# Partial sums of a chunked matmul: two of four groups start on empty PSUM banks and are added in DRAM

## The chip, the cores and the metric

One Trainium2 chip, one of its cores. A time is device microseconds of one execution of the whole program; the time of a kernel is the median over its runs. One execution was also profiled, and all rows below come from that one.

## The reference, cut to what matters

Sigmoid attention (4 batches, 12 heads, 448 tokens, head size 64) gives 1792 tokens of 768. Two feed-forward blocks follow, all in float32:

```python
rms = np.sqrt(np.mean(x * x, axis=-1, keepdims=True) + 1e-06)
xn = x / rms * rms_g                                 # 1792 x 768
g, val = xn @ w_gate, xn @ w_val                     # 768 -> 1536
x = (g / (1 + np.exp(-g)) * val) @ w_out             # 1536 -> 768
h = x @ w_in2                                        # 768 -> 2048
out = (h - np.tanh(h)) @ w_out2                      # 2048 -> 768
```

The last product, with `w_out2`, is the one that the change touches.

## The kernel before

Activations lie transposed: a tile holds 128 features by the 448 tokens of one batch. Float32 values are split into a high and a low part, and a product of one 128x128 weight block with one tile is three matmuls of 448 columns (high x high, high x low, low x high). TensorE's order in the feed-forward part is fixed in the text: all its pieces are in one stream ("moe"). The phases are A (gate and value), B (`w_out`), C (`w_in2`) and D (`w_out2`). A and C take two batches at a time with a seven-product scheme (line 734); B and D use line 769. The batches go in two pairs, (0, 1) and then (2, 3).

Phase D has 16 key chunks (features of the 2048) and 6 output chunks `m`. Its keys are cut into four groups of four (`GR["D"]`), because the activations of a group are made by the C pieces just before it and their tiles are used up before the next. So D runs as group 0, two C pieces, group 1, two C pieces, group 2, one C piece, group 3. For one pair of batches each group makes 6 x 2 partial sums of 128x448. The order inside a group is chunk `m` after chunk `m`, both batches side by side, one PSUM bank each.

- `prologue` (line 639) begins a sum. In group 0 it takes an empty bank. In a later group it loads the sum so far from DRAM (line 644, a transfer that SyncE issues, `unit<-sumD`) and `seed` (line 647) copies it into the bank: the copy runs on ScalarE or VectorE under line 279, as all plain copies do, and is shown as `ps<-unit`.
- The first matmul of a group starts the bank anew only in group 0 (`k < GR[ph]`); in the others it adds to the seed.
- `epilogue` (line 650) copies the bank to a unit in SBUF (line 279, `unit<-ps`). After groups 0 to 2 SyncE stores that to DRAM (line 657, `sumD<-unit`); after group 3 it goes to the output (line 660).

So there are 3 x 12 x 2 = 72 loads, seeds and stores of this kind in D. Phase B has two groups and 24 of each.

Everything is recorded as a piece of work with the engines that may do it and a cost for each, and the class `Plan` then chooses the engine and the order of issue. It walks through a model of the five engines' clocks, takes among the pieces that can start soonest the oldest one, and looks at most 500 pieces ahead (`WINDOW`). Buffers are handed out in that modelled order too: 74 units of 128x448 in SBUF and 8 PSUM banks. Each engine then runs its list strictly in order on the chip, waiting on semaphores for what a piece reads. A transfer's cost in the model is the time that the issuing engine is taken, and `after` the time from there to its landing. `pool` and `dve` (lines 272 to 276) also mark operations that the model does not let VectorE and GpSimd do at the same time (the flag behind the cost).

Other work that shares the engines in phase D: weight blocks of `w_in2` and `w_out2` are loaded (line 329), unpacked (lines 279 and 339), summed (385), split in two (279 and 350) and, for the second pair of batches, stored and reloaded (370 and 419). The results of C pass through `tanh` (685), a subtraction (686) and a split (279 and 635). From the last C piece of the first pair on, the normalised input of the second pair is made (`spread_norm`, `x_units`: 572, 576, 580, 623, 595, 600).

Of the kernel before, what the change touches and what calls it, by code (L numbers as in the profile page):

```python
# [15 lines left out]
ALU = mybir.AluOpType  # L16
# [3 lines left out]
B, H, S, D = 4, 12, 448, 64  # L20
# [5 lines left out]
GR = {"B": 6, "D": 4}  # L26
# [34 lines left out]
class Plan:  # L61
# [11 lines left out]
    def add(self, engines, run, reads=(), writes=(), stream=None, after=0):  # L73

        n = len(self.work)
        self.work.append((engines, run, tuple(reads), tuple(writes), stream, after))
        self.rank.append(n + self.later)
        for s, _ in (*reads, *writes):
            if not s.uses or s.uses[-1] != n:
                s.uses.append(n)  # L80
# [134 lines left out]
def tile_sigmoid_attention_moe_moe(  # L215
# [14 lines left out]
    nc = tc.nc  # L230
# [20 lines left out]
    add = plan.add  # L251
# [4 lines left out]
    def bank(kind="mm"):  # L256
        return slot(kind, ps_p, [P, 512], F32, "ps")

    def unit(kind, dt=F32):
        return slot(kind, unit_p, [P, S], dt, "unit")  # L260
# [4 lines left out]
    def keys(c):  # L265
        return [c["h"]["t"], c["l"]["t"]]


    def act(n, psum=False, ptr=False):
        return {"ACT": ((155 if psum else 195) + n / 1.2, False)}  # L270

    def dve(n, two=True, psum=True, fast=False):
        return {"DVE": ((150 if psum or fast else 210) + n / 0.96 / (2 if fast else 1), fast or (two and not psum))}
# [4 lines left out]
    def copy(engines, to, of, reads, writes):  # L278
        add(engines, lambda e: (nc.scalar.copy if e == "ACT" else nc.vector.tensor_copy)(to(), of()), reads, writes)  # L279
# [323 lines left out]
    def right_units(ph, bs, i, x):  # L603

        f = {}
        split_of = lambda n: lambda: right_split(ph, bs, n, i, f[n])

        def of(e, names):
            f.update(zip(names, (x[b, 2 * i + e] for b in bs)))

        def total(n, a, b):
            f[n] = right_sum(f[a], f[b])

        return ([lambda: (of(0, ("B11", "B12")), split_of("B11")()), lambda: total("T1", "B12", "B11"), split_of("T1")],
                [lambda: (of(1, ("B21", "B22")), split_of("B21")()), lambda: total("T2", "B22", "T1"), split_of("T2"),
                 lambda: total("T3", "B22", "B12"), split_of("T3"), lambda: total("T4", "B21", "T2"), split_of("T4"), split_of("B22")])
# [11 lines left out]
    ps_t, gs_t, sums_t = {}, {}, {}  # L628
    last_group = lambda ph: {"B": KF1, "D": KF2}[ph] // GR[ph] - 1

    def parts(t):
# [4 lines left out]
            c["l"].tile, t.tile, c["h"].tile.bitcast(F32)), [t["t"], kh], [kl])  # L636
        return c

    def prologue(ph, bs, m, g):
        for b in bs:  # L640
            ps = ps_t[ph, b, m] = bank("m2")
            if g:
                d, a = sums_t.pop((ph, b, m)), unit("acc")
                add({"SP": (650, False)}, lambda e, a=a, d=d: nc.sync.dma_start(out=a.tile, in_=d.tile), [d["t"]], [a["t"]], after=2000)
                seed(ps, a, False)

    def seed(to, of, psum):
        copy({**act(S, psum=psum), **dve(S)}, lambda: to.tile[:, :S], lambda: of.tile[:, :S], [of["t"]], [to["t"]])

    def epilogue(ph, bs, b, m, g):  # L650
        ps = ps_t.pop((ph, b, m))
        last = g == last_group(ph)
        a = unit("sum" if last else "st")
        copy({**act(S, psum=True), **dve(S)}, lambda: a.tile, lambda: ps.tile[:, :S], [ps["t"]], [a["t"]])
        if not last:
            d = sums_t[ph, b, m] = Slot(None, lambda: dram_p.tile([P, S], F32, name=f"sum{ph}{b}_{m}_{g}"))
            add({"SP": (650, False)}, lambda e: nc.sync.dma_start(out=d.tile, in_=a.tile), [a["t"]], [d["t"]], after=2000)
            return
        if ph == "D":
            add({"SP": (650, False)}, lambda e: nc.sync.dma_start(out=out[b, m], in_=a.tile), [a["t"]], [], after=2000)  # L660
            return
        xg[b, m] = a
        if b == bs[-1]:
            if m % 2 == 0:
                halves["C", bs, m // 2] = right_units("C", bs, m // 2, xg)
            for u in halves["C", bs, m // 2][m % 2]:
                u()
# [82 lines left out]
    def job_units(j):  # L750

        ph, bs, _, blocks = jobs[j]
        if blocks is None:
            return seven_units(j)

        def one(n, k, m):
            w = whls[j]
            first, last = k % GR[ph] == 0, k % GR[ph] == GR[ph] - 1
            if first:
                prologue(ph, bs, m, k // GR[ph])  # L760
            pss = [ps_t[ph, b, m] for b in bs]
            acs = [acts[ph, b, k] for b in bs]
            part = lambda p: w.tile[:, "hl".index(p), n * P:(n + 1) * P]

            def block(e):
                hi, lo = part("h"), part("l")
                for i, (wt, p) in enumerate(((hi, "h"), (hi, "l"), (lo, "h"))):
                    for ps, a in zip(pss, acs):
                        nc.tensor.matmul(  # L769
                            ps.tile[:, :S], lhsT=wt, rhs=a[p].tile,  # L770
                            start=first and i == 0 and k < GR[ph], stop=last and i == 2, skip_group_check=True)

            add({"PE": (3 * len(bs) * MM, False)}, block,
                [w["h"], w["l"], *[k for a in acs for k in keys(a)]], [ps["t"] for ps in pss], stream="moe")
            if last:
                for b in bs:
                    epilogue(ph, bs, b, m, k // GR[ph])

        return [lambda n=n, k=k, m=m: one(n, k, m) for n, (k, m) in enumerate(blocks)]
# [170 lines left out]
```

## Time and profile before

| | |
|---|---|
| median of 3 runs | 1110.64 us (1110.25 to 1111.54) |
| the profiled execution | 1111.01 us |
| its span in the trace | 1109.2 us |

The span runs from the first to the last instruction of the program in the trace; 1.8 us of the profiled execution lie outside it. "Busy" is the union of an engine's instructions; register, wait and transfer-issuing instructions do not count as busy, except that what GpSimd issues stands under POOL. PE is TensorE, PEld its weight loads, DVE is VectorE, ACT is ScalarE, POOL is GpSimd, SP is SyncE, and a "q" behind an engine's name is its sequencer.

### The profile page before, as it was taken

Reading aid. Unit: us, or ns where it says so; the run is one execution under the profiler, and the core shown is the slowest. Engines: PE = TensorE matmul, PEld = TensorE weight load, DVE = VectorE, ACT = ScalarE, POOL = GpSimd, SP = SyncE. Lnnn points to the kernel's source line nnn. Section 1 sums busy time; section 2 is a strip of 40 time slices with the busy share of each in tenths; the row PEclk is TensorE's granted clock in tenths of the full one; section 3 lists DMA queues with packets and bytes.
Section 4 is the critical chain, followed back from the end, with each engine's and each line's share of the span. In section 5 each row is a group of like instructions: output and inputs, shape, how many; then the busy total and the mean of one; then the engine's idle time right before and its main releaser. Section 6 shows DMA issues by size and latency. Waiting matters only on the chain.

```text
span 1109.2 us, 14723 instructions
## 1 busy us (share of the span) xinstructions
PE 1092.8 (99%) x5364; PEld 914.3 (82%) x5364; DVE 701.0 (63%) x1075; ACT 503.2 (45%) x896; POOL 149.6 (13%) x108
## 2 busy tenths in 40 slices
PE   9999999999999998999999999999999999999998
PEld 3333338999999997999998888999899989999997
DVE  0353816877478789767698966633666686474651
ACT  5776864443255346355364533312344353243431
POOL 0000003300021000123132001200021021222100
PEclk9999999999999999999999999999999999999999
DMA  5774554469668546599899563334344135656432
GB/s 163 246 221 114 143 177 179 146 253 316 212 207 282 208 157 232 181 321 364 288 345 320 192 198 119 115 121 135 103 164 147 57 103 159 195 179 199 146 116 100
DMA packets 92456, 211.40 MB, mean 191 GB/s; under 512 B 25312, under 2 KB 58080, under 8 KB 92384
## 3 DMA queue, kind: packets, MB, share of 16 engines
q1 hardware_dynamic: 92080, 210.30, 56.3%
q8 instruction: 42, 0.69, 0.3%
q14 instruction: 30, 0.25, 0.1%
q10 hardware_dynamic: 304, 0.16, 0.1%
HBM read 137.68 MB, written 72.74 MB: 190 GB/s over the span
## 4 chain that ended last, share of the span: by engine, by line
PE 94%; DVE 4%; issue 1%; ACT 1%; DMA 0%; POOL 0%; DVEq 0%; ACTq 0%; POOLq 0%
PE ps L734 42%; PE ps L769 37%; PE ps L490 7%; PE ps L520 7%; DVE unit L279 1%; DVE wt L350 1%; DVE unit L635 1%; PE ps L286 1%; DVE unit L708 0%; ACT unit L279 0%; DVE unit L681 0%; PE ps L554 0%; DMA wC<-cv 0%; ACT wt L279 0%; DVE unit L600 0%
## 5 line engine op out<-in xcount | busy, mean ns | idle before, releaser
L734 PE MATMUL ps<-unit,wt 128*128 128x448 f32 x2520 | 521.5, 366 | 9.6 <-DVE unit L708 5.4
L734 PEld LDWEIGHTS ps<-unit,wt 128*128 128x128 f32 x2520 | 471.4, 188 | 55.7 <-DVE unit L708 6.9
L769 PE MATMUL ps<-unit,wt 128*128 128x448 f32 x2016 | 413.9, 365 | 1.1 <-ACT wt L279 1.1
L769 PEld LDWEIGHTS ps<-unit,wt 128*128 128x128 f32 x2016 | 378.1, 188 | 33.1 <-ACT wt L279 1.5
L279 ACT COPY unit<-ps 128x448 f32<-128x448 f32 x172 | 91.2, 534 | 329.0 <-PE ps L769 200.5
L279 DVE COPY unit<-ps 128x448 f32<-128x448 f32 x80 | 49.9, 624 | 129.8 <-PE ps L769 124.0
L350 DVE TENSOR_TENSOR wt<-cv,wt 128x768 fp32r<-128x768 f32 (+1 forms) x111 | 101.7, 924 | 18.8 <-ACT wt L279 17.4
L279 ACT CAST wt<-cv 128x768 fp32r<-128x768 f32 (+1 forms) x97 | 75.1, 781 | 41.4 <-PE ps L734 16.3
L497 ACT ACTIVATE unit<-ps 128x448 f32<-128x448 f32 (+1 forms) x192 | 86.5, 547 | 5.9 <-PE ps L490 5.9
L635 DVE TENSOR_TENSOR unit<-unit 128x448 fp32r<-128x448 f32 x94 | 75.8, 807 | 7.4 <-ACT unit L279 4.7
L490 PE MATMUL ps<-wt 64*128 64x448 f32 (+1 forms) x384 | 78.9, 547 | 0.0
L520 PE MATMUL ps<-unit,vs 128*64 128x448 f32 (+1 forms) x384 | 77.7, 545 | 0.0
L350 POOL TENSOR_TENSOR wt<-cv,wt 128x768 fp32r<-128x768 f32 (+1 forms) x25 | 48.2, 1928 | 214.9 <-ACT wt L279 145.5
L708 DVE TENSOR_TENSOR unit<-ps,unit 128x448 f32<-128x448 f32 x84 | 51.9, 619 | 33.2 <-PE ps L734 23.7
L350 POOL TENSOR_TENSOR wt<-wt 128x768 fp32r<-128x768 f32 (+1 forms) x21 | 36.3, 1732 | 269.6 <-ACT wt L279 188.9
L279 ACT CAST wt<-wt 128x768 fp32r<-128x768 f32 (+1 forms) x60 | 44.8, 753 | 53.8 <-PE ps L734 38.0
L339 DVE SCALAR_TENSOR_TENSOR cv<-wt,zero 128x768 uint32<-128x768 uint32 x68 | 66.8, 982 | 2.5 <-ACT unit L535 0.7
L490 PEld LDWEIGHTS ps<-wt 64*128 64x128 f32 (+1 forms) x384 | 32.3, 173 | 43.3 <-issue 36.1
L520 PEld LDWEIGHTS ps<-unit,vs 128*64 128x64 f32 (+1 forms) x384 | 25.2, 136 | 49.1 <-issue 32.9
L279 ACT CAST zero<-wt 128x768 f16<-128x768 bf16 x49 | 53.1, 1083 | 26.6 <-DVE cv L339 19.8
L279 ACT CAST unit<-unit 128x448 fp32r<-128x448 f32 x91 | 51.3, 567 | 25.4 <-DVE unit L681 9.0
L350 DVE TENSOR_TENSOR wt<-wt 128x768 fp32r<-128x768 f32 (+1 forms) x59 | 51.4, 879 | 6.4 <-ACT wt L279 5.5
(49 smaller groups left out, 548.9 us busy)
## 6 DMA issues: line engine op xcount, KB each, us to landing
wt<-in_w_out SPq DMA_DIRECT2D x28, 768.0 KB, 5.9
sumD<-unit SPq DMA_DIRECT2D x72, 224.0 KB, 2.7
unit<-sumD SPq DMA_DIRECT2D x72, 224.0 KB, 4.7
wt<-in_w_in SPq DMA_DIRECT2D x16, 768.0 KB, 5.8
wC<-cv SPq DMA_DIRECT2D x32, 384.0 KB, 4.3
wt<-wC SPq DMA_DIRECT2D x16, 768.0 KB, 4.3
wt<-in_w_gate SPq DMA_DIRECT2D x12, 768.0 KB, 5.2
wt<-in_w_val SPq DMA_DIRECT2D x12, 768.0 KB, 5.4
```

What stands on the lines that cost most here:

```text
L279: add(engines, lambda e: (nc.scalar.copy if e == "ACT" else nc.vector.tensor_copy)(to(), of()), reads, writes)
L286: nc.tensor.matmul(ps[:, :S], lhsT=mark[:, :P], rhs=mark, start=True, stop=True)
L339: add(dve(NW, psum=False), lambda e: nc.vector.scalar_tensor_tensor(out=c.tile.bitcast(U32), in0=r.tile[:, :NW, 1], scalar=13, in1=z.tile, ...
L350: add({**dve(n, psum=False), **pool(n)}, lambda e: ENG[e].tensor_sub(lo(), of(), hi().bitcast(F32)), [*reads, *kh], [*kl])
L490: nc.tensor.matmul(ps[i, c].tile[:n, :S], lhsT=t.tile[rows, at:at + n], rhs=t.tile[rows, :S], start=True, stop=True)
L497: add(act(S, psum=True), lambda e: nc.scalar.activation(to.tile[at:at + n, :S], ps.tile[:n, :S], AF.Sigmoid, bias=-math.log(S), scale=1.0 ...
L520: nc.tensor.matmul(ps.tile[i * D:(i + 1) * D, :S], lhsT=v.tile[:n, c, i, :], rhs=a[c][i].tile[:n, :], start=(c == 0), stop=(c == 3))
L635: add({**pool(S), **dve(S, psum=False)}, lambda e: ENG[e].tensor_sub(c["l"].tile, t.tile, c["h"].tile.bitcast(F32)), [t["t"], kh], [kl])
L708: add(dve(S), lambda e: nc.vector.tensor_add(t.tile, ps.tile[:, :S], t.tile), [ps["t"], t["t"]], [t["t"]])
L734: nc.tensor.matmul(ps.tile[:, :S], lhsT=part(a), rhs=x[b].tile, start=n in ((1, 2, 5) if opening else (1, 5)) and i == 0 and q == 0, stop= ...
L769: nc.tensor.matmul(ps.tile[:, :S], lhsT=wt, rhs=a[p].tile, start=first and i == 0 and k < GR[ph], stop=last and i == 2, skip_group_check=True)
```

## The change

Groups 1 and 2 of phase D no longer load and seed the sum so far; their first matmul starts the bank anew, as in group 0. Their epilogue still copies the bank to a unit, and then GpSimd issues a transfer that adds the unit to the sum in DRAM (`accum_op=ALU.add`). Group 0's sum is stored as before, and group 3 loads the sum and seeds with it as before. In the model of `Plan` the adding transfer takes GpSimd for 1100 ns and lands 3000 ns later; a SyncE store takes 650 and 2000. Phase B, with two groups, is as it was, since its second group is its last.

```diff
+    def seeded(ph, g):
+        return g and (ph != "D" or g == last_group(ph))
+
     def prologue(ph, bs, m, g):
         for b in bs:
             ps = ps_t[ph, b, m] = bank("m2")
-            if g:
+            if seeded(ph, g):
                 d, a = sums_t.pop((ph, b, m)), unit("acc")
                 add({"SP": (650, False)}, lambda e, a=a, d=d: nc.sync.dma_start(out=a.tile, in_=d.tile), [d["t"]], [a["t"]], after=2000)
                 seed(ps, a, False)
@@ epilogue
         copy({**act(S, psum=True), **dve(S)}, lambda: a.tile, lambda: ps.tile[:, :S], [ps["t"]], [a["t"]])
+        if not last and g:
+            d = sums_t[ph, b, m]
+            add({"POOL": (1100, False)}, lambda e: nc.gpsimd.dma_start(
+                out=d.tile, in_=a.tile, accum_op=ALU.add), [a["t"], d["t"]], [d["t"]], after=3000)
+            return
         if not last:
@@ block, in one
-                            start=first and i == 0 and k < GR[ph], stop=last and i == 2, skip_group_check=True)
+                            start=first and i == 0 and not seeded(ph, k // GR[ph]), stop=last and i == 2, skip_group_check=True)
```

## Rows read from the trace of the kernel before

**Rows 1.** The page: busy time, share of the span and instructions by engine

```profile
PE 1092.8 (99%) x5364; PEld 914.3 (82%) x5364; DVE 701.0 (63%) x1075; ACT 503.2 (45%) x896; POOL 149.6 (13%) x108
```

**Rows 2.** Stretches of the span (us): busy and count by engine, clock, DMA share, GB/s

```profile
490.00:594.00 104.00, 104.00 (x513) 96.01 (x512) 80.47 (x122) 52.84 (x88) 28.03 (x16) 1.00 0.93 332
594.00:611.00 17.00, 15.48 (x74) 13.40 (x73) 16.57 (x25) 10.10 (x18) 6.32 (x4) 1.00 0.93 318
611.00:640.00 29.00, 27.85 (x137) 25.20 (x136) 27.34 (x48) 16.22 (x31) 0.00 (x0) 1.00 0.57 187
640.00:676.00 36.00, 34.60 (x169) 31.08 (x168) 25.31 (x37) 14.31 (x26) 3.68 (x2) 1.00 0.51 169
...
894.00:1067.00 173.00, 173.00 (x855) 160.03 (x854) 104.35 (x156) 62.84 (x110) 36.83 (x25) 1.00 0.52 169
```

**Rows 3.** Who TensorE waited for from 490 us on: total us, times, longest

```profile
PE ps L734 <- DVE unit L708: 1.5, 1, 1.5
PE ps L734 <- DVE unit L279: 1.4, 2, 0.7
PE ps L734 <- ACT unit L279: 1.2, 2, 0.6
PE ps L769 <- ACT wt L279: 1.1, 1, 1.1
```

**Rows 4.** Groups of instructions, 490 to 594 us: the seeds (count | busy, mean ns | idle before)

```profile
L279 ACT COPY ps<-unit 128x448 f32<-128x448 f32 x17 | 8.9, 534 | 3.4 <-DMA unit<-sumD 3.0 <-DVE unit L279 0.3
L279 DVE COPY ps<-unit 128x448 f32<-128x448 f32 x7 | 4.3, 625 | 1.2 <-DMA unit<-sumD 1.1
```

**Rows 5.** The same groups, 955 to 1063 us

```profile
L279 DVE COPY ps<-unit 128x448 f32<-128x448 f32 x13 | 7.7, 622 | 0.2
L279 ACT COPY ps<-unit 128x448 f32<-128x448 f32 x11 | 5.8, 536 | 0.1
```

**Rows 6.** The page's DMA issues: count, KB each, median us from issue to landing

```profile
sumD<-unit SPq DMA_DIRECT2D x72, 224.0 KB, 2.7
unit<-sumD SPq DMA_DIRECT2D x72, 224.0 KB, 4.7
```

**Rows 7.** What the SyncE queue waited for, 960 to 1072 us

```profile
SPq L419 <- POOL wt L350: 24.7, 5, 8.3
...
SPq L644 <- DMA sumD<-unit: 3.6, 3, 2.9
```

**Rows 8.** Timeline from 593.8 us: the end of group 2 of the first pair

```profile
593.84 0.54 ACT L279 COPY unit<-ps 128x448 f32<-128x448 f32 x1 [1.28 <-PE ps L769]
...
594.40 1.08 SPq L657 DMA_DIRECT2D sumD<-unit  x2
594.52 0.62 DVE L279 COPY unit<-ps 128x448 f32<-128x448 f32 x1
594.75 1.81 POOL L350 TENSOR_TENSOR wt<-cv,wt 128x768 fp32r<-128x768 f32 x1 [9.93 <-DVE wt L279]
```

**Rows 9.** Groups of instructions, 506 to 598 us: GpSimd, and VectorE work beside it

```profile
L350 POOL TENSOR_TENSOR wt<-cv,wt 128x768 fp32r<-128x768 f32 x11 | 21.4, 1947 | 58.9 <-DVE wt L279 23.5 <-ACT wt L279 21.5 <-DMA wC<-cv 13.9
...
L635 DVE TENSOR_TENSOR unit<-unit 128x448 fp32r<-128x448 f32 x12 | 10.8, 901 | 0.5 <-ACT unit L279 0.2
L279 DVE CAST unit<-unit 128x448 fp32r<-128x448 f32 x5 | 3.6, 724 | 0.2
```

**Rows 10.** The stretch of groups 1 and 2 of the first pair, columns as in 2

```profile
506.00:594.00 88.00, 88.00 (x435) 81.28 (x434) 69.17 (x103) 42.82 (x71) 21.23 (x12) 1.00 0.91 326
```

**Rows 11.** Timeline of VectorE and GpSimd, 560 to 569 us (start, us, what)

```profile
560.47 0.39 DVE L279 CAST unit<-unit 128x448 fp32r<-128x448 f32 x1
...
565.64 0.62 DVE L635 TENSOR_TENSOR unit<-unit 128x448 fp32r<-128x448 f32 x1
...
566.75 1.88 POOL L350 TENSOR_TENSOR wt<-cv,wt 128x768 fp32r<-128x768 f32 x1 [4.17 <-ACT wt L279]
566.83 2.04 DVE L279 CAST unit<-unit 128x448 fp32r<-128x448 f32 x1
```

## Prediction

> **What bounds the kernel now.** I read the page first: TensorE is busy 99% of the span, and VectorE, the next, 63% [rows 1]. So only what makes TensorE wait can move the time, and I asked next how its idle time lies over the stretches. Groups 1 and 2 of phase D lie between 490 and 594 us for the first pair of batches and inside 894 to 1067 us for the second. In both TensorE is busy for the whole of the stretch, 104.00 of 104 us and 173.00 of 173 us [rows 2]. Since "busy" is a union of overlapped matmuls it could hide short gaps, so I divided: 104 us by 513 matmuls is 202.7 ns and 173 us by 855 is 202.3 ns. Two stretches with very different side work run at one pace, at a granted clock of 1.00, so there is no hidden wait to win back.
>
> The idle time stands just behind the first of them: 1.52 us from 594 to 611, 1.15 us from 611 to 640 and 1.40 us from 640 to 676, together 4.07 us. From 594 to 640 VectorE is the crowded engine, 16.57 of 17 and 27.34 of 29 us [rows 2]. There the normalised input of the second pair is made beside the last group of D. The list of waits says the same: from 490 us to the end TensorE waits 5.2 us (1.5 + 1.4 + 1.2 + 1.1), none for a seed or a partial sum, most of it for VectorE [rows 3].
>
> **The change part by part.** The planner is a list scheduler that walks the program in order, so before the pieces that are gone come within its sight, near 490 us, I expect the old order. TensorE's own order is fixed in the text and its matmuls stay the same in number; only a flag of the first ones changes.
>
> Removed: 48 seeds. The trace has 17 on ScalarE and 7 on VectorE for the first pair, 8.9 + 4.3 us [rows 4], and 11 and 13 for the second, 5.8 + 7.7 us [rows 5]: 26.7 us of side-engine time. All of it lies where TensorE never waits, so on the path it is worth 0. What hides it: matmuls already queued on other banks. Could the freed time help the crowded stretch behind 594 us? In 490 to 594 VectorE has 23.5 of 104 us idle as it is [rows 2], so the work behind 594 us is not held back by a lack of VectorE time before; freeing 4.3 us more there buys 0 of the 4.07 us by itself. The bound from the other side is the whole 5.2 us of later waits [rows 3].
>
> Removed too: 48 loads, and 48 plain stores become adding transfers. A load takes 4.7 us and a store 2.7 us to land [rows 6]; nobody on TensorE's path waits for either. The traffic hardly changes by my reading: a load and a store together bring 224 KB out of HBM and 224 KB into it, and so does an addition in DRAM. The DMA engines are at 0.93 of their time in the first stretch [rows 2], so this matters: if an addition took more of them than the load and store it replaces, weights would land late. No row has such a transfer. From below I set its landing at a store's 2.7 us, from above at load plus store, 7.4 us, and take the upper, since it has to read the sum and write it.
>
> Moved: the wait for the copied sum goes from SyncE's queue to GpSimd's. SyncE's queue gets lighter. What stands behind the waiting instruction on GpSimd are weight splits (line 350), and SyncE's reloads of weights wait for those already, 24.7 us in 5 waits [rows 7], without TensorE feeling it (173.00 of 173). How long GpSimd is taken per addition the trace does not tell. Bounds: 0.54 us, a SyncE issue (two in 1.08 us) [rows 8], and 1.95 us, GpSimd's own weight split [rows 9]. I take 1.1 us, the planner's figure, which is near their middle. For 24 additions that is 26 us in the 88 us of the first pair's groups 1 and 2, where GpSimd is busy 21.23 us [rows 10]: 54%. It would be full at (88 - 21.2) / 24 = 2.8 us each, beyond the upper bound. So GpSimd does not become the bound.
>
> Its company with VectorE is the real question. GpSimd's split at 566.75 us ran 1.88 us, and a VectorE cast that started beside it took 2.04 us and ended with it; the same cast alone takes 0.39 us [rows 11]. A GpSimd instruction can thus hold VectorE for its whole length. Over 506 to 598 us I count what was lost: line 635, 12 x (901 - 620) ns = 3.4 us, and the casts, 5 x (724 - 390) ns = 1.7 us, 5.1 us in all beside 21.4 us of GpSimd splits [rows 9, 11], a quarter. The planner's flag keeps apart operations that collide, but the addition is entered without that flag. If an addition holds VectorE as a split does, 24 of them cost 24 x 1.1 x 0.24 = 6.3 us of VectorE, less than its 18.8 us idle (88 - 69.17) [rows 10]. That cover ends at 594 us: the last two output chunks' four additions come from copies just before (594.38 and 595.14 us are the ends of the last two) [rows 8] and run into the crowded stretch. Expected there 4 x 1.1 x 0.24 = 1.1 us of VectorE; at worst, all four held for 1.95 us, 7.8 us; at best 0. TensorE's waits there are partly for ScalarE, so I let half of the expected part through: +0.5 us. For the second pair the stretch behind is not crowded (104.35 of 173 us) and the cost is 0.
>
> The Trainium skill speaks against this change: "SBUF — State Buffer", section "Who interferes with whom", says that VectorE's two-port modes and GpSimd lock each other out, whichever came first, and that a transfer issued from GpSimd is held up when it can't write its descriptors meanwhile. The held cast [rows 11] agrees for a GpSimd tensor instruction; no row here shows it for a transfer. By that rule the additions are issued late and VectorE is held; without it the term above is 0 and the forecast 1110.6.
>
> Sum: 0 for the seeds, 0 for SyncE, 0 for GpSimd's load, +0.5 us: 1111.01 becomes 1111.5 in the profiled execution. That one stands 0.4 us above the median, so the median goes from 1110.64 to 1111.1 us.
>
> **Rivals.** Slower, one: the hold at 594 us decides. Four additions hold VectorE for their full 1.1 us and the crowd passes it on: +4.4 us, 1115.0. It counts from 0.56 us each on the path (2.2 / 4). For it: the held cast [rows 11], and VectorE's 0.43 us of slack in 594 to 611. Against it: only a quarter was lost so far. It is also what the rule of the Trainium skill above would do.
>
> Slower, two: additions land late. The last group's loads already wait for the landing of a store, 3.6 us in 3 waits [rows 7]; with 7.4 us of landing against the planner's 1.1 + 3.0 each could be 3.3 us later and hold the reloads queued behind on SyncE, or the unit's next writer. If TensorE feels one, 1114. Against it: today a load takes 4.7 us [rows 6] where the planner reckons 2.0, and TensorE feels nothing of it.
>
> Faster: the planner, with 26.7 us of side work gone, orders the crowded stretch otherwise and most of its 4.07 us goes: -3 us, 1107.6. It counts when at least 2.2 us go. For it: the waits there are matters of order more than of capacity. Against: the last group's seeds and the second pair's input work, which fill it, stay. The same reshuffle can as well add a wait.
>
> **How the numbers follow.** About 0.2% (2.2 us) is what a measurement of this kernel can tell from no change. Forecast, within it: 0.49. Hold at 594 us: 0.20. Late landings: 0.07. A worse order after 490 us, by 2 to 4 us: 0.05. Faster by a better order: 0.19. So faster 0.19, same 0.49, slower 0.32. The range is 1108.0 to 1115.0: its low end takes in a part of the faster case (2.6 us gone), its high end the hold at its full 1.1 us; what exceeds it needs splits' 1.95 us or a late transfer more than once.
>
> **What would show it.** Right: 48 fewer seeds and loads, TensorE still busy throughout 490 to 594 and 894 to 1067 us, its waits between 594 and 676 us near 4 to 5 us. The hold would show as VectorE casts of 1 us and more beside POOL transfers, and a longer wait near 609 us. Late landings would show as waits of SyncE's loads for `sumD`. Wrong would be a TensorE wait inside groups 1 and 2, or GpSimd taken 2.8 us or more per addition.

## The result and the profile after

The changed kernel ("after" from here on) takes 1119.39 us (median of 4 runs, 1119.02 to 1119.94) against 1110.74 us for the kernel before beside it (4 runs, 1110.25 to 1111.54): 8.65 us more, ratio 1.0078 with a 95% interval of 1.006 to 1.0095. That is slower, and above the range of 1108.0 to 1115.0. The profiled execution took 1119.18 us, its span is 1117.4 us. The diff has moved line 734 to 742, 769 to 777, 708 to 716 and the load of a sum from 644 to 647; the addition is line 660.

First the page of after: busy time by engine, the two DMA queues (packets, MB, share of 16 engines), what moved in HBM, and the additions' landing.

```profile
PE 1095.6 (98%) x5364; PEld 916.1 (82%) x5364; DVE 687.8 (62%) x1059; ACT 491.4 (44%) x875; POOL 172.8 (15%) x145
...
q1 hardware_dynamic: 78256, 188.28, 50.7%
q0 software_dynamic: 6912, 11.01, 6.6%
...
HBM read 126.67 MB, written 72.74 MB: 178 GB/s over the span
...
sumD<-unit POOLq DMA_DIRECT2D x48, 224.0 KB, 6.8
```

The seeds went as foretold: VectorE has 13.2 us less and ScalarE 11.8 us less [rows 1], 25.0 us where the seeds took 26.7. TensorE is busy 2.8 us longer with the same matmuls, and the rest is idle time. Where, the windows say (columns as in [rows 2]):

```profile
490.00:594.00 104.00, 104.00 (x514) 96.07 (x513) 70.81 (x115) 46.33 (x74) 34.70 (x30) 1.00 0.93 268
594.00:611.00 17.00, 9.98 (x43) 8.25 (x42) 8.37 (x16) 5.76 (x12) 6.16 (x7) 0.89 1.01 247
611.00:640.00 29.00, 27.86 (x128) 24.65 (x128) 24.92 (x41) 18.43 (x34) 1.84 (x1) 0.95 0.56 196
...
902.00:1075.00 173.00, 173.00 (x853) 159.89 (x852) 102.89 (x149) 56.02 (x97) 52.85 (x45) 1.00 0.54 135
```

All of the loss lies from 594 to 640 us. Groups 1 and 2 of the first pair are still full (104.00 of 104 us), and so are the second pair's, 8 us later than before (173.00 of 173 us). From 594 to 611 us the three computing engines all do less than before, while the DMA engines are full (1.01) and move 247 GB/s, not 318. The list of waits from 490 us to the end has one new wait of 7.0 us:

```profile
PE ps L742 <- ACT unit L279: 8.7, 4, 7.0
PE ps L777 <- ACT wt L279: 1.1, 1, 1.1
PE ps L742 <- DVE unit L279: 0.7, 1, 0.7
```

I laid the two traces side by side, matmul by matmul. Up to 602.6 us the pace is the same; there after is 7.17 us late at one matmul, then the next twelve cost it another 2.0 us, and 1.6 us come back because the work behind the 1.5 us wait of before [rows 3] is done by then. With small differences behind it the end is 8.1 us later. The 2.0 us are the clock; the windows around the pause (a matmul that crosses an edge counts in both windows):

```profile
600.00:602.70 2.70, 2.70 (x14) 2.19 (x12) 1.15 (x3) 0.00 (x0) 0.40 (x1) 1.00 1.04 160
609.70:612.00 2.30, 2.23 (x6) 2.04 (x7) 0.00 (x0) 0.91 (x2) 0.06 (x1) 0.50 1.05 430
612.00:614.20 2.20, 2.20 (x8) 1.96 (x7) 1.57 (x3) 2.20 (x5) 0.84 (x1) 0.52 0.99 386
614.20:618.00 3.80, 3.80 (x20) 3.25 (x19) 3.70 (x6) 1.80 (x5) 1.00 (x1) 1.00 0.85 323
```

Before the pause the granted clock is 1.00 (2.4 GHz); after 7.0 us without a matmul it is 0.50 (1.2 GHz), and from about 614.2 us it is 1.00 again. In between, from 609.77 to 614.28 us, 12 matmuls take 4.51 us, 2.07 us more than 12 x 0.203.

What ScalarE waited for is read from the timeline of after (start, us, what, idle before and its releaser):

```profile
592.34 0.54 ACT L279 COPY unit<-ps 128x448 f32<-128x448 f32 x1
...
593.17 1.16 POOL L660 DMA_DIRECT2D sumD<-unit  x1 [0.51 <-ACT unit L279]
...
595.96 1.40 ACT L279 COPY unit<-ps 128x448 f32<-128x448 f32 x3 [3.08 <-PE ps L576]
596.79 3.61 POOL L660 DMA_DIRECT2D sumD<-unit  x4 [2.46 <-ACT unit L279]
...
598.59 3.63 SPq L647 DMA_DIRECT2D unit<-sumD  x6
...
604.00 0.62 DVE L600 TENSOR_TENSOR unit<-unit 128x448 f32<-128x448 f32 x1 [2.85 <-DMA sumD<-unit]
...
604.18 0.54 ACT L279 COPY ps<-unit 128x448 f32<-128x448 f32 x1 [5.50 <-DMA unit<-sumD]
...
607.74 1.51 ACT L279 COPY ps<-unit 128x448 f32<-128x448 f32 x3 [1.28 <-DMA unit<-sumD]
...
609.19 0.52 ACT L279 COPY unit<-ps 128x448 f32<-128x448 f32 x1
```

And the same instructions in the timeline of before:

```profile
591.84 0.97 SPq L644 DMA_DIRECT2D unit<-sumD  x2
...
597.80 1.67 ACT L279 COPY ps<-unit 128x448 f32<-128x448 f32 x3
...
601.12 0.53 ACT L279 COPY unit<-ps 128x448 f32<-128x448 f32 x1
```

Read it backwards. TensorE wants the copy that ScalarE does at 609.19 us (before: 601.12). Ahead of it in ScalarE's list, as before, stand five seeds of group 3, and these wait 5.50, 1.22 and 1.28 us for their loads. The first load was issued at 598.59 us (before: 591.84), because SyncE had stood 4.4 us for an addition to land: the one issued at 593.17 us, which reads the very unit that the load is to fill. The other 2.4 us are its place in the list: it stands behind one more store of packed weights, which waited for VectorE. SyncE's waits in after, 588 to 611 us:

```profile
SPq L370 <- DVE cv L339: 9.0, 2, 5.8
SPq L647 <- DMA sumD<-unit: 4.4, 1, 4.4
```

Once issued, the six loads take 5.5 to 8.2 us, 2.9 to 4.0 before. The fifth seed is the last ahead of the copy, and its load decides: issued at 600.54 us (before: 596.68), landed at 608.59 (before: 600.58). So 3.9 us of late issue and 4.1 us of slower landing make up the 8.1 us by which the copy is late, of which TensorE had 1.0 us of slack. The copies before 598 us are late by the same way: those at 580.58, 590.97, 592.34 and 595.96 us go into units whose additions, by the trace's semaphores, landed at 580.50, 590.87, 592.13 and 595.58 us.

The units are not short when this happens. By the buffers' places in the built program and the times of the trace 73 or all of the 74 units hold something from 574.5 to 585.5 us, but only 58 at 594.1 us and 52 at 598.4 us. A unit's next writer is fixed with the lists, though, so SyncE stands for its own unit while others are empty.

The additions' landings, by the view of the sums' transfers from 505 to 600 us (min/median/max; three loads are among them), and who waited for any of these:

```profile
L660 POOL DMA_DIRECT2D sumD<-unit x24: 863/1178/1987, 518.0 to 598.4; - x24
...
  ACT ps L279: 8.0, 3
  DVE unit L279: 3.9, 1
  DVE unit L600: 2.9, 1
  DVE unit L572: 2.3, 2
...
DMA to landing us min/median/max: 3.8/8.0/12.3
```

Why they land late: the DMA view from 566 to 611 us (packets, MB, share of 16 engines; KB each and median us to landing), of before,

```profile
q1 hardware_dynamic: 6418, 14.88, 93.9%
...
sumD<-unit SPq DMA_DIRECT2D x12, 224.0 KB, 2.6
```

and of after:

```profile
q1 hardware_dynamic: 3108, 9.13, 57.3%
q0 software_dynamic: 1728, 2.75, 40.8%
...
sumD<-unit POOLq DMA_DIRECT2D x12, 224.0 KB, 7.9
```

Twelve additions take 40.8% of 45 us, 1.53 us of all 16 engines each. The page's queue rows price what they replace: q1's share of the span went from 56.3% of 1109.2 us to 50.7% of 1117.4 us, 58.0 us for 48 pairs, so a load and a store together cost 1.21 us. The page of before:

```profile
q1 hardware_dynamic: 92080, 210.30, 56.3%
```

Twelve times 0.32 us is 3.9 us more in a stretch that had (1 - 0.94) x 45 = 2.7 us free. By this working it is over-full, and the weights and loads in it are late too. But the full stretch is only a part of an addition's lateness: in after the second pair's 24 additions, at a DMA share of 0.54, still take 6.5 us at the median. Nor is lateness enough for a loss: group 1's twelve of the first pair take 9.4 us at the median, and TensorE stays busy beside them.

### The profile page after: what moved, and what is told of

It reads as the page before. It is cut to its first block, busy times and chain, and to the rows that moved or that the text cites. A ratio compares the mean times of both kernels' runs of the same rounds, so it can differ in the third digit from the quotient of the medians.

```text
span 1117.4 us, 14624 instructions
## 1 busy us (share of the span) xinstructions
PE 1095.6 (98%) x5364; PEld 916.1 (82%) x5364; DVE 687.8 (62%) x1059; ACT 491.4 (44%) x875; POOL 172.8 (15%) x145
## 3 DMA queue, kind: packets, MB, share of 16 engines
q1 hardware_dynamic: 78256, 188.28, 50.7%
q0 software_dynamic: 6912, 11.01, 6.6%
HBM read 126.67 MB, written 72.74 MB: 178 GB/s over the span
## 4 chain that ended last, share of the span: by engine, by line
PE 95%; DVE 2%; DMA 1%; ACT 1%; issue 1%; POOL 0%; ACTq 0%; DVEq 0%; POOLq 0%
PE ps L742 43%; PE ps L777 37%; PE ps L490 7%; PE ps L520 7%; DMA unit<-sumD 1%; PE ps L286 1%; DVE wt L350 1%; DVE unit L635 1%; DVE unit L279 1%; ACT unit L279 0%; DVE unit L716 0%; PE ps L576 0%; DVE unit L689 0%; PE ps L554 0%; DMA wC<-cv 0%
## 5 line engine op out<-in xcount | busy, mean ns | idle before, releaser
L279 DVE COPY unit<-ps 128x448 f32<-128x448 f32 x75 | 46.8, 624 | 136.8 <-PE ps L777 126.6
L350 DVE TENSOR_TENSOR wt<-cv,wt 128x768 fp32r<-128x768 f32 (+1 forms) x116 | 104.9, 912 | 19.4 <-ACT wt L279 17.6
L350 POOL TENSOR_TENSOR wt<-wt 128x768 fp32r<-128x768 f32 (+1 forms) x19 | 32.6, 1716 | 266.0 <-ACT wt L279 191.0
L350 POOL TENSOR_TENSOR wt<-cv,wt 128x768 fp32r<-128x768 f32 (+1 forms) x20 | 38.2, 1911 | 186.2 <-ACT wt L279 141.2
L279 ACT CAST unit<-unit 128x448 fp32r<-128x448 f32 x96 | 54.0, 567 | 25.0 <-DVE unit L689 9.1
```

The lines of the kernel that those rows point to most:

```text
L350: add({**dve(n, psum=False), **pool(n)}, lambda e: ENG[e].tensor_sub(lo(), of(), hi().bitcast(F32)), [*reads, *kh], [*kl])
```

## Experiments

Each ran beside the kernel before on its chip; the ratio is to that one (medians 1111.19 to 1111.31 us), with its 95% interval. Of TensorE's waits the longest from 490 us on is told. The diffs are cut to the lines that matter.

**One pair of batches alone.** The first pair loads and seeds as before.

```diff
-        return g and (ph != "D" or g == last_group(ph))
+        return g and (ph != "D" or bs != BATCHES[1] or g == last_group(ph))
```

> The change is made for the second pair of batches alone; the first pair keeps its loads and seeds. Theory 'late landing': the 8.7 us come from one place, the end of group 2 of the first pair, where ScalarE stands in its list behind seeds whose loads come late; the second pair gains and loses nothing. Expected 1110.7 us, within 1 us of the kernel before. Rival 'GpSimd and VectorE hold each other': each addition costs a little wherever it is, half of them remain, so about half the loss, 1115 us.

1110.84 us, 0.9999 (0.999 to 1.0008), longest wait 1.3 us. The 24 additions of the second pair cost nothing and save nothing, though they take 6.1 us at the median to land: TensorE stays busy beside them (180.00 of 180 us from 900 to 1080 us), so no wait behind them reaches it. The loss is in the first pair.

**The same transfers as plain stores, and none at all.** Plan's lists are the same as in after in both.

```diff
-                out=d.tile, in_=a.tile, accum_op=ALU.add), ...
+                out=d.tile, in_=a.tile), ...
```

> Every engine's list is that of the changed kernel; the 48 transfers of GpSimd only store and do not add, so the sums of groups 0 and 1 are lost. Theory 'late landing, because an addition is slow': a plain store of GpSimd lands in 2 to 4 us instead of a median of 6.8, the loads of group 3 are issued near 594 instead of 598.6 us, and TensorE's wait of 7.0 us shrinks to under 2 us: 1110 to 1113 us. Rival 'late because GpSimd issues it': landings stay above 5 us and the time stays at 1118 to 1119.5 us. Rival 'the order': the time stays at 1119.

```diff
-            add({"POOL": (1100, False)}, lambda e: nc.gpsimd.dma_start(
-                out=d.tile, in_=a.tile, accum_op=ALU.add), ...
+            add({"POOL": (1100, False)}, lambda e:
+                None, ...
```

> The lists of the changed kernel with the 48 transfers of GpSimd left out, so the partial sums of groups 1 and 2 are lost; their copies to SBUF stay. Theory 'late landing': nothing lands late, the loads of group 3 wait for nothing and TensorE's wait of 7.0 us is gone: 1109 to 1112 us. This is also what the taken seeds and loads are worth by themselves, which I expect to be nothing that can be told from the kernel before. Rival 'the order': the seeds of group 3 stand ahead of the copy that TensorE needs in ScalarE's list in any case, so the wait stays and the time is 1117 or more.

Plain: 1112.72 us, 1.0011 (1.0002 to 1.0021). Left out: 1111.25 us, 1.0000 (0.9991 to 1.0009). With the lists of after and no transfer the loss is gone, so neither the order nor GpSimd's place in it is a cause by itself; and 48 loads, seeds and stores fewer gain nothing, with the DMA share from 490 to 594 us down from 0.93 to 0.68. Issued plainly from the same place, the transfers cost 1.5 us by the medians, 1.2 by the ratio. The DMA view from 566 to 611 us of the plain version:

```profile
q1 hardware_dynamic: 4384, 11.63, 72.3%
q0 software_dynamic: 768, 2.75, 15.3%
...
sumD<-unit POOLq DMA_DIRECT2D x12, 224.0 KB, 6.7
```

15.3% of 45 us by 12 is 0.57 us each, against 1.53 us as an addition. The addition of the same 2.75 MB has 1728 packets, not 768. One half of the theory missed: the plain stores land in 6.7 us at the median, not in 2 to 4, where SyncE's of before took 2.6. So in this stretch a part of the lateness comes with GpSimd's transfers, adding or not; in the second pair's they take 3.5 us. The two whose units the next copy and the first load of group 3 take, issued at 589.75 and 591.12 us, landed in 2.6 and 2.2 us, and the first load of group 3 went out at 593.46 us, near the 594 us that was foretold.

**The planner told of the real landing.**

```diff
-... [a["t"], d["t"]], [d["t"]], after=3000)
+... [a["t"], d["t"]], [d["t"]], after=9000)
```

> The changed kernel, but the planner is told that an addition lands 9000 ns after its issue instead of 3000. Theory 'late landing': the buffers and the sums come free in the plan when they do on the chip, so the loads and seeds of group 3 are put further back in the lists and TensorE's long wait goes: 1110 to 1113 us. Rival 'the additions load the DMA engines so much that any order waits': 1116 us or more.

1120.47 us, 1.0078 (1.0061 to 1.0095): no cure. The wait has moved. TensorE's longest wait, and VectorE's instruction before it:

```profile
PE ps L576 <- DVE unit L572: 6.3, 1, 6.3
```

```profile
600.86 1.59 DVE L572 TENSOR_SCALAR unit<-id_sb,rc 112x112 f32<-112x112 f32 x8 [3.61 <-issue]
```

The view names no releaser for those 3.61 us; the unit that line 572 writes was last read by the addition issued at 595.08 us, which landed at 600.78 us. So another engine's list now stops at a unit that its plan had meant to be free. The addition took 5.7 us, less than the 9 that the model was told: what the plan had wrong here is when the addition comes, not how long it takes. That was not followed further.

**Additions from buffers of their own.** Their units come from a pool of 4 (70 stay in common), then 6 (68).

```diff
-N_UNIT, ... = 74, ...
+N_UNIT, ... = 70, ...
+    own_p = ctx.enter_context(tc.tile_pool(name="own", bufs=4))
-        a = unit("sum" if last else "st")
+        a = unit("sum" if last else "st") if last or not g else slot("own", own_p, [P, S], F32, "own")
```

> The units that the additions read get four buffers of their own, in the planner and in SBUF, and the common pool has 70 units instead of 74; the planner's order changes somewhat with it. Theory 'buffers': what turns a late landing into TensorE's wait is that a unit read by an addition is handed at once to the next copy, load or input tile, which then waits for the landing. With buffers of their own only the additions' next copies wait, four additions back. Expected: the loads of group 3 no longer wait for a landing, 1111 to 1114 us. Rival 'DMA engines': the additions load the DMA engines so much that weights and sums come late in any case, 1116 us or more. Against me stands that 70 common units may be too few, which would show as waits on TensorE's results, not on landings.

> The same with six buffers for the additions and 68 common units. Theory 'buffers': the copies at the end of group 2 wait for an addition six back instead of four, so less than with four buffers, 1110 to 1113 us, if 68 common units are enough. Rival 'DMA engines': no better than with four, 1116 us or more.

Four: 1117.7 us, 1.0056 (1.0041 to 1.0071). Six: 1121.63 us, 1.0091 (1.0073 to 1.0108), with a wait of 4.1 us for line 572's counterpart. With four, SyncE issues the first load of group 3 at 595.04 us, 3.55 us sooner than in after, but the loads take 4.3 to 10.3 us. No load of group 3 waits for an addition any more; SyncE now stands for the packed weights ahead of them in its list. SyncE's longest wait from 580 to 625 us, then who waited for whom from 590 to 611 us:

```profile
SPq L372 <- DVE cv L341: 9.7, 2, 7.1
```

```profile
ACT ps L281 <- DMA unit<-sumD: 5.9, 4, 3.5
...
PE ps L744 <- ACT unit L281: 4.1, 1, 4.1
```

So four buffers give back 2.3 us and six nothing. The planner's order changes with both, so by themselves these two do not price the hand-on of the unit; why six are worse than four was not followed further.

**Which twelve additions.** First group 2 of the first pair stores plainly and the other 36 add; then only those twelve add.

```diff
-                out=d.tile, in_=a.tile, accum_op=ALU.add), ...
+                out=d.tile, in_=a.tile, **({} if g == 2 and bs == BATCHES[0] else {'accum_op': ALU.add})), ...
```

> Every engine's list is that of the changed kernel; only the twelve transfers of group 2 of the first pair store plainly instead of adding, so that group's sums replace the earlier ones. Theory 'late landing at one place': the time is lost by these twelve alone, so it is that of the kernel in which all 48 store plainly, 1112 to 1113.5 us. Rival 'every addition costs a share of the DMA engines': three quarters of the loss stay, 1117 us.

> The lists of the changed kernel again; only the twelve transfers of group 2 of the first pair add, the other 36 store plainly, so the sums of group 1 and of the second pair are not complete. Theory 'late landing at one place': the whole loss is there, 1118 to 1120 us. Rival 'every addition costs a share': about a quarter of the loss, 1113 to 1114 us.

36: 1113.03 us, 1.0009 (1.0 to 1.0019), longest wait 1.1 us. Only the twelve: 1118.92 us, 1.0068 (1.0053 to 1.0083), longest wait 7.3 us. So twelve transfers carry the loss.

**Room on the DMA engines.** Nine stores of packed weights between 565 and 594 us are left out, and the second pair loads other pieces in their place.

```diff
-        add({"SP": (1100, False)}, lambda e: nc.sync.dma_start(out=d.tile[:, at], in_=c.tile), ...
+        add({"SP": (1100, False)}, lambda e: None if d in gone() else nc.sync.dma_start(out=d.tile[:, at], in_=c.tile), ...
```

> The lists of the changed kernel, but nine plain weight stores of SyncE between 565 and 594 us are left out (the four of C's last piece and five of w_out2's), and the second pair loads other pieces' weights in their place, so its results are not those of the reference. All additions stay. Theory 'DMA engines': additions land late because the engines are full in this stretch; with 3.5 MB less in it they land sooner, the loads of group 3 come earlier and TensorE's wait of 7.0 us falls below 3 us, 1111 to 1115 us. Rival 'an addition is slow by itself': landings and wait stay, 1118 to 1119.5 us.

1114.92 us, 1.0030 (1.0017 to 1.0044), longest wait 2.3 us. Most additions of the stretch now land in 3.8 to 7.9 us, and the loads of group 3 begin at 593.68 us. SyncE stood 13.8 us for an addition ahead of the first, so here it is the sooner landing that lets them go. That gives back 5.0 of the 8.65 us. The last two additions, issued right behind six loads of group 3, still take 8.9 and 10.4 us.

**Seeds that wait for nothing.** The seeds of group 3, first pair, copy zeros; all transfers stay.

```diff
-                seed(ps, a, False)
+                seed(ps, a, False, ph == "D" and bs == BATCHES[0])
...
-... lambda: of.tile[:, :S], ...
+... lambda: mark if zero else of.tile[:, :S], ...
```

> The lists of the changed kernel with all transfers, but the seeds of group 3 of the first pair copy a tile of zeros that is always in SBUF instead of the loaded sum, so the sums of that pair's groups 0 to 2 are lost. Theory 'ScalarE stands in its list behind the seeds': additions and loads land as late as before, but nobody on TensorE's path waits for them, and the wait of 7.0 us is gone, 1110 to 1112.5 us. Rival 'late transfers reach TensorE by other ways too' (weights, units that additions still read): 1115 us or more.

1120.59 us, 1.0079 (1.0062 to 1.0096): nothing came back. But this run changes more than it was meant to: a loaded unit without a reader is handed on while its load is still under way. From 590 to 611 us:

```profile
ACT unit L279 <- DMA sumD<-unit: 12.5, 3, 9.5
...
PE ps L742 <- ACT ps L279: 4.8, 1, 4.8
ACT unit L580 <- DMA unit<-sumD: 4.7, 1, 4.7
```

ScalarE now stands directly for additions (9.5 us at the longest) and for a load into units that it is to write. It does not tell what the seeds' wait alone is worth; it shows that it is not needed for the loss.

**Both halves at once**, the four buffers and the left-out weight stores together (the two diffs above).

> Both halves of the cause at once. The copied sums that are to be added have four buffers of their own (70 are left in common), and the nine plain weight stores of 565 to 594 us are left out (that part of the computation is gone: the second pair loads other weight pieces in their place). Theory that the loss has two parts which stack, transfers that land late because the DMA engines are full, and common units that are handed on while such a transfer still reads them: alone the first removal gave 4.5 us back and the second 1.7, so both give 6 to 8, 1111 to 1113.5 us, and TensorE waits under 2 us between 594 and 611 us. Rival that it is one cause, the full engines, and that the units of its own add nothing: 1114.5 to 1116 us. Rival that the twelve additions cost something by themselves, whatever is around them: 1116 us and over.

1110.93 us, 1.0000 (0.9991 to 1.001). All of it is back. TensorE's waits and the window behind group 2:

```profile
PE ps L744 <- ACT unit L281: 1.6, 3, 0.6
PE ps L744 <- DVE unit L718: 1.2, 1, 1.2
```

```profile
594.00:611.00 17.00, 15.85 (x75) 13.68 (x74) 14.43 (x24) 10.95 (x21) 6.21 (x5) 1.00 0.96 299
```

The additions are all there, on GpSimd, at 0.9 to 1.2 us of issue. So an addition costs TensorE nothing by itself, and the one-cause rival (full engines alone, 1114.5 to 1116) falls.

The first load shows why the parts do not add up. With the buffers alone it goes out at 595.04 us, held by the packed weights ahead of it; with the stores left out alone at 593.68, held by an addition; with both at 589.46, held by neither. The fifth seed follows it: 600.65 us before, 608.73 after, 606.96, 602.36 and 599.23 in these three. So leaving out the stores takes two things away, the load on the DMA engines and their place ahead of the loads in SyncE's list, and this run does not price them one by one. Leaving out transfers is no gain of its own here: without the 48 the time was 1111.25 us.

**All but those twelve**, a whole kernel: group 2 of the first pair loads, seeds and stores as before, the other three places add.

```diff
-        return g and (ph != "D" or g == last_group(ph))
+        return g and (ph != "D" or g == last_group(ph) or (g == 2 and bs == BATCHES[0]))
```

> The best version that the runs so far point to: empty banks and additions in three of the four places, and in group 2 of the first pair loads and seeds and plain stores as before. Theory that the loss lies in those twelve additions alone and that the freed seeds are worth nothing: 1110.4 to 1112.0 us, no different from before, and TensorE waits about 5 us from 490 us on, as before. Rival that group 1 of the first pair loses too, as its transfers lie in the same full stretch: 1113 us and over. Rival that freed engines do help once the late additions are gone: under 1109 us.

1111.56 us, 1.0001 (0.9991 to 1.001), and TensorE's waits from 490 us on are 5.9 us in the same four kinds as before, 1.8 us the longest. The rival that group 1 of the first pair loses too falls with this run: its twelve additions land in 8.6 us at the median beside a DMA share of 0.94 (490 to 594 us) and cost nothing. A full stretch and a late landing do not make the loss alone; it takes a next writer on TensorE's path.

Safe in three places, then, and of use in none: no version here beats the kernel before.

## Why the prediction was wrong

**The step that failed** is the one on the removed loads and moved stores: "nobody on TensorE's path waits for either", hence "0 for SyncE". It measured 8.1 us (1119.39 us with the transfers, 1111.25 without them). Three things in it were wrong, the third above all.

- The condition was named, "if an addition took more of them than the load and store it replaces, weights would land late", and then put aside by counting bytes. Bytes were not the measure: an addition takes 1.53 us of the 16 engines, the pair 1.21. In a stretch at 0.93 to 0.95 that difference had no room, and half of what made the critical copy late is the slower landing of the load before it.
- The landing was bounded at 7.4 us, a load plus a store in a median case, and taken as a bound. The view shows 8.0 us median and 12.3 us at the most. Two medians added are no bound. As a size it was near: the median of all 48 is 6.8 us. It was the wait that was missing from the sum, more than the landing.
- "Nobody waits" was read from the list of waits of before, where the landing was 2.7 us. But the next writer of a unit waits until the transfer that reads it has landed, and which writer is next is fixed with the lists. With the landing three times as long the waits appeared: SyncE's load (4.4 us), whose queue was counted as lighter, the copies, and the work of lines 572 and 600.

**The rival "slower, two"** had this mechanism, down to "the reloads queued behind on SyncE, or the unit's next writer", and its sign in the trace, waits of SyncE's loads for `sumD`, came. It had a chance of 0.07 and one delay of 3.3 us, 1114. Measured were three in a row (late copy, late load, slow load) and then 2.0 us of half clock, which no term held. What was set against it, that a load takes 4.7 us and is planned with 2.0, compared a transfer that other buffers cover with one that holds a buffer.

**The likeliest loss, the hold of VectorE**, did not happen. Its second sign, a longer wait near 609 us, came, but with another cause: the copy on ScalarE. VectorE and GpSimd in after from 506 to 598 us:

```profile
L635 DVE TENSOR_TENSOR unit<-unit 128x448 fp32r<-128x448 f32 x12 | 7.9, 661 | 0.4
...
L279 DVE CAST unit<-unit 128x448 fp32r<-128x448 f32 x3 | 1.2, 394 | 0.2
```

```profile
L660 POOL DMA_DIRECT2D sumD<-unit x23 | 20.8, 1104 | 21.1 <-ACT unit L279 17.9 <-DMA wt<-in_w_out 3.2
```

With 23 additions in the stretch both VectorE lines are nearer to their free-running 620 and 390 ns than before [rows 9], as fewer splits run on GpSimd (6 where there were 11). So the +0.5 us term measured nothing. The rule of the Trainium skill ("SBUF — State Buffer", "Who interferes with whom") that a transfer issued from GpSimd is held up by VectorE's two-port work shows no price here either: issues took 0.86 to 1.99 us in a stretch where VectorE was two thirds busy, and in the version that lost nothing 0.86 to 1.22 us. The four above 1.25 us are the last ones of additions issued in a row, and one of them (1.52 us) has no VectorE instruction beside it; whether VectorE made the others longer was not tried.

**Right were** the seeds at 0 on the path (left-out version, 1.0000), GpSimd's load (0.9 to 1.2 us for most additions where 1.1 was taken, not the 2.8 us at which it fills), and 0 for the second pair (0.9999). The rival of a better order did not come: with the transfers out of the way TensorE's idle time from 594 to 676 us stayed, 3.5 us in the windows of the left-out version for 4.07 before, and the time was 1111.25 us.

**How far it is shown.** Runs show that twelve additions carry the loss, that it is in their landing and not in the order or the issue alone, and that it is gone when the nine stores are left out and the additions have four buffers. How the 8.65 us split is not a fixed sum: alone the first gave 5.0 and the second 2.3 us back, together all. What of the first is room on the DMA engines and what is SyncE's shorter list, and what of the second is the planner's other order, stays open. That the clock's 2.0 us follow from the pause is read from the windows, not tried by itself. Why GpSimd's plain stores land later than SyncE's in the full stretch, and why an addition takes 2.7 times a plain store's share, stays open; its packets are 2.25 times as many.

## What to carry to other kernels

Before a transfer of a new kind goes into a stretch, ask what share of the DMA engines it takes and what is free there, and not how many bytes it moves. A full stretch alone cost nothing here in group 1, so then ask what buffer it holds until it has landed, and which in-order list has that buffer's next writer, even if other buffers are empty: a wait that the profile of before does not show can be one longer landing away. Work that is off the critical path is worth nothing when it is removed, but its replacement can still put itself on the path.

## What was not expected of the hardware

- An addition of 224 KB into DRAM takes 1.53 us of the 16 DMA engines, a plain store issued from the same place 0.57 us, a load and a store by SyncE 1.21 us together. It has 144 packets, the plain store 64. The page's HBM line does not count an addition's reading: reads fell by the 11.01 MB of the 48 loads, 137.68 to 126.67 MB.
- All queues share the engines: from 566 to 611 us 57.3% and 40.8% make 98%, and the SyncE loads of sums in that stretch took 7.7 us at the median where they took 3.9. That agrees with the Trainium skill ("DMA: Bandwidth & Descriptors", "Issuing engines are not separate DMA queues"), which says that transfers of all issuers run on the same 16 engines and interleave.
- Additions of one size landed 3.8 us after their issue at best and 12.3 us at worst in one kernel; at a DMA share of 0.54 the median was 6.5 us. Plain stores from GpSimd took 6.7 us at the median from 566 to 611 us, where SyncE's of before took 2.6, and 3.5 us from 900 to 1080 us.
- After 7.0 us without a matmul TensorE's granted clock was 0.50 from 609.7 us to about 614.2 us, then 1.00.
